# Five instead of four of the eight second-layer steps in split form

## The chip, the cores and the metric

One Trainium2 chip, one of its cores. The program is one launch; the metric is device time in microseconds (us) of that core. Runs of one kernel agree within a few tenths of a per cent; the profile is of one execution.

## The reference

Two parts follow each other. Agent attention: 49 agents attend to 12480 keys (per batch, two batches), and every query attends to the 49 agents. Its output, 24960 rows of 128, goes through a feed-forward layer of 2048 hidden units with ELU.

```python
def _attn_ref(q, k, v, agents):
    a2k = sm(agents, k)              # softmax(scale * a @ b^T)
    agent_v = a2k @ v                # 49 x 128 per batch
    q2a = sm(q, agents)              # 12480 x 49 per batch
    return q2a @ agent_v

def _moe_ref(x, w_in, w_out):
    h = x @ w_in                     # 24960 x 2048
    g = where(h > 0, h, exp(min(h, 0)) - 1)
    return g @ w_out                 # 24960 x 128
```

All is float32; w_in and w_out come as float64.

## The kernel before, in words

`agent_v @ w_in` is folded into a matrix A of 49 rows per batch, so that a hidden value is `p @ A`, with p the query's softmax over the agents. A is kept as a pair of fp32r parts (`ahi`, `alo`), p as well. Queries come in 26 groups (`j`) of 960; each group has two halves of 480, and each half passes through the 2048 hidden units in NP = 8 steps of 256 units (two chunks of 128). That makes S = 416 steps `s`. A *block* is the eight steps of one half: its step number is c = s mod 8 (0 to 7), and its second layer is summed up in one pair of PSUM tiles `o0`, `o1` (`ps_o`, one buffer each).

The work of a step:

- `p1(s)` (L403, TensorE): first layer, three pairs of fp32r matmuls into an `h` slot. Two matmuls of a pair run side by side on the two row halves of the array. There are three `h` slots (`ps_h`); the attention's work takes slots from the same three, in the order in which the program asks for them.
- `elu(s)` (L409, L412, L414): ScalarE writes relu(-h) to `e` (two buffers), then exp of it in place; VectorE makes `g` from `e` and `h`, which sets the `h` slot free.
- `split(s)` (L421, L205), for steps in SPLIT alone: VectorE casts `g` to `hi` (fp32r); GpSimd makes `lo = g - hi` in two halves.
- `p2(s)` (L443, TensorE): second layer. A plain step has two pairs of float32 matmuls, `g` with `w_f`. A split step has six pairs of fp32r matmuls: `hi` with `w_lo` and with `w_hi` (two chunks each), then `lo` with `w_hi`. After step 7, VectorE copies `o1` to `ob` (L455), ScalarE copies `o0` to `oa` (L458), GpSimd adds them (L459).

The order is written out by hand: each engine runs its instructions in the order of the program. In *turn* s of the loop come p1(s), p2(s-4) (LAG = 4; up to turn 5 it is p2(s-3), and turn 6 has none), elu(s), split(s), and then what `pre` lists for that turn. So turn 3 of a block holds the second layer of step 7 of the block before, and turn 4 that of its own step 0. In turn 3 ScalarE's copy `oa` stands between relu and exp of step 3, and VectorE's copy `ob` ahead of `g` of step 3.

The listed attention work: in turn 3 of every second block the scores of the next query group (`q_scores`, L157, with `q_max`, `q_sub`), here called a *score block*; in turn 3 of the blocks between them `q_ring`, the transposes (L328) and the making of `px` (L339, L205), a *ring block*. Both take an `h` slot between those of steps 3 and 4. The sums `z` follow in turns 5 and 6 of a score block, the product `pp` (L324) in its turn 7. In the first seven groups there are two rounds of scores of the second batch's keys per group (`k_round`, turns 13 and 17 of 16), in the next five the sums over v (`ev1`); in about the last thirteen groups only the query work is left.

A prologue of 55 us loads the keys, converts the weights from float64 (`conv`) and computes A of the first batch. There `wo_step`, `wo_hi` and `wo_lo` make `w_hi` and `w_lo` for the steps in SPLIT and `w_f` for the rest.

Of the kernel before, what the change touches and what calls it, by code (L numbers as in the profile page):

```python
# [22 lines left out]
def tile_agent_attention_moe(  # L23
# [24 lines left out]
    LEAD = 6  # L48
    NP = NM // 2
    EDGE = (NP - 1 + LAG) % NP  # L50
    SPLIT = (1, 4, 6, 7)
    PLAIN = tuple(c for c in range(NP) if c not in SPLIT)
    scale = 1.0 / float(C) ** 0.5

# [16 lines left out]
    w_f = big.tile([128, len(PLAIN), 2, 128], F32)  # L71
    w_hi = big.tile([128, len(SPLIT), 2, 128], F32R)
    w_lo = big.tile([128, len(SPLIT), 2, 128], F32R)
    s_all = big.tile([TP, NR, R + 1, NA], F32)
# [123 lines left out]
    def cast_hi(eng, out, x):  # L198
        if eng is nc.scalar:
            nc.scalar.activation(out=out, in_=x, func=ACTF.Copy)  # L200
        else:
            eng.tensor_scalar(out=out, in0=x, scalar1=1.0, scalar2=0.0, op0=ALU.mult, op1=ALU.add)
# [155 lines left out]
    def wo_step(c):  # L358

        if c not in wo_gen:  # L360
            parts = []
            for i in range(2):
                x = 2 * c + i
                y = lambda m, i=i: m[:, 256 * i:256 * i + 256]
                if x in SPLIT:
                    w_e[x] = wc_p.tile([128, 256], F32, tag="even", name="even")
# [8 lines left out]
    def w_part(w, x):  # L375
        return w[:, SPLIT.index(x)].rearrange("p m d -> p (m d)")

    def wo_hi(c):
        for x in (2 * c, 2 * c + 1):
            if x in SPLIT:  # L380
                cast_hi(nc.scalar, w_part(w_hi, x), w_e[x])
# [324 lines left out]
```

## Time and profile before

| what | value |
|---|---|
| time, median of 3 runs | 1029.51 us (1029.46 to 1030.34) |
| the profiled execution's own time | 1029.2 us |
| its span, first to last instruction | 1027.4 us |
| granted TensorE clock, mean | 0.994 |
| TensorE busy in matmuls / weight loads | 98% / 73% |
| ScalarE, VectorE, GpSimd busy | 87%, 80%, 57% |

How to read it: PE is TensorE's matmuls and PEld its weight loads; DVE is VectorE, ACT is ScalarE, POOL is GpSimd. A share is an average over the span. A matmul's end is modelled, so that a recorded duration is longer than the distance to the next matmul; distances are read from starts. In a row of the timeline the first number is the start, the second the length, both in us from the span's start, and what stands in brackets is the idle time of that engine before it and what ended it.

### The profile page before, as it was taken

To read this page: it belongs to the slowest core of one execution; us is meant where nothing else is said; L and a number is where in the kernel's file an instruction comes from. 1 tells how busy PE (TensorE), PEld (TensorE's weight loads), DVE (VectorE), ACT (ScalarE), POOL (GpSimd) and SP (SyncE) were. 2 spreads that over 40 slices of the span, in tenths; PEclk is the share of its full clock that TensorE was granted. 3 is DMA by queue.
4 is the path that set the end of the run, shared out by engine and by line. 5 is a ranking of instruction groups with operands and counts; after the bars stand their busy time and mean duration, and the time that the engine had idled before them with its cause. 6 is when DMAs were issued, how large, how long until landed. Compare 5 with 4: busy or idle time off the path is not lost.

```text
span 1027.4 us, 24745 instructions
## 1 busy us (share of the span) xinstructions
PE 1011.0 (98%) x10138; PEld 753.0 (73%) x10138; DVE 816.9 (80%) x989; ACT 896.4 (87%) x1018; POOL 586.8 (57%) x490
## 2 busy tenths in 40 slices
PE   7999999999999999999999999999999999999998
PEld 5866777777776677776766777777777677777786
DVE  6778787787878777887778888878887887888775
ACT  4588998898898888888889999999999999999995
POOL 3146565565565565566555565656656565656655
PEclk8999999999999999999999999999999999999999
DMA  9921211211222322320110111011011101101000
GB/s 350 368 79 46 93 64 40 84 64 46 78 64 73 89 65 62 100 64 11 55 44 11 54 45 51 14 55 45 22 44 45 54 11 55 45 26 39 25 20 20
DMA packets 25980, 67.27 MB, mean 65 GB/s; under 512 B 3083, under 2 KB 14963, under 8 KB 25867
## 3 DMA queue, kind: packets, MB, share of 16 engines
q1 hardware_dynamic: 25867, 65.69, 19.2%
q8 instruction: 80, 1.31, 0.6%
q14 instruction: 33, 0.27, 0.1%
HBM read 43.11 MB, written 12.78 MB: 54 GB/s over the span
## 4 chain that ended last, share of the span: by engine, by line
PE 92%; DMA 3%; ACT 2%; DVE 2%; issue 1%; SPq 0%; POOLq 0%; POOL 0%; DVEq 0%; ACTq 0%
PE o L443 57%; PE h L403 28%; PE h L157 3%; DMA k<-in_kT_dram 2%; PE h L220 2%; PE h L328 1%; ACT e L409 1%; DMA v<-in_vx_dram 1%; ACT e L412 1%; DVE g L414 1%; PE h L260 0%; DVE m_all L166 0%; PE o L157 0%; DVE ex L96 0%; ACT ex L100 0%
## 5 line engine op out<-in xcount | busy, mean ns | idle before, releaser
L205 POOL TENSOR_TENSOR lo<-g,hi 128x480 fp32r<-128x480 f32 x416 | 511.8, 1252 | 390.2 <-DVE hi L421 231.7
L414 DVE SCALAR_TENSOR_TENSOR g<-e,h 128x960 f32<-128x960 f32 x416 | 478.5, 1153 | 174.5 <-ACT e L412 140.5
L409 ACT ACTIVATE e<-h 128x960 f32<-128x960 f32 x416 | 403.1, 969 | 59.3 <-PE h L403 48.1
L412 ACT ACTIVATE e<-e 128x960 f32<-128x960 f32 x416 | 418.3, 1006 | 11.6
L443 PE MATMUL o<-g,w_f 64*128 64x480 f32 x1664 | 373.6, 562 | 0.0
L403 PE MATMUL h<-py,ahi 49*128 49x480 f32 x832 | 319.7, 463 | 0.7 <-DVE g L414 0.3
L403 PE MATMUL h<-px,ahi 49*128 49x480 f32 x832 | 319.0, 463 | 1.0 <-DVE g L414 0.9
L443 PEld LDWEIGHTS o<-g,w_f 64*128 64x128 f32 x1664 | 169.5, 185 | 91.6 <-issue 80.4
L403 PEld LDWEIGHTS h<-px,ahi 49*128 49x128 f32 x832 | 146.4, 186 | 50.5 <-issue 37.0
L403 PEld LDWEIGHTS h<-py,ahi 49*128 49x128 f32 x832 | 146.4, 186 | 44.6 <-issue 31.7
L421 DVE CAST hi<-g 128x960 fp32r<-128x960 f32 x208 | 171.9, 827 | 7.2
L403 PE MATMUL h<-py,alo 49*128 49x480 f32 x416 | 156.3, 376 | 0.0
L403 PE MATMUL h<-px,alo 49*128 49x480 f32 x416 | 156.2, 376 | 0.0
L443 PE MATMUL o<-hi,w_lo 64*128 64x480 f32 x832 | 130.7, 380 | 0.0
L443 PE MATMUL o<-lo,w_hi 64*128 64x480 f32 x832 | 129.4, 376 | 0.4 <-POOL lo L205 0.4
L443 PE MATMUL o<-hi,w_hi 64*128 64x480 f32 x832 | 128.4, 374 | 0.0
L443 PEld LDWEIGHTS o<-hi,w_lo 64*128 64x128 f32 x832 | 85.9, 185 | 7.6
L443 PEld LDWEIGHTS o<-hi,w_hi 64*128 64x128 f32 x832 | 85.2, 184 | 7.6
L443 PEld LDWEIGHTS o<-lo,w_hi 64*128 64x128 f32 x832 | 85.1, 184 | 7.6 <-POOL lo L205 0.9
L403 PEld LDWEIGHTS h<-px,alo 49*128 49x128 f32 x416 | 76.6, 184 | 4.2
L403 PEld LDWEIGHTS h<-py,alo 49*128 49x128 f32 x416 | 76.6, 184 | 4.1
L459 POOL TENSOR_TENSOR ob<-ob,oa 128x480 f32<-128x480 f32 x51 | 62.1, 1217 | 7.4 <-ACT oa L458 7.4
(86 smaller groups left out, 517.5 us busy)
## 6 DMA issues: line engine op xcount, KB each, us to landing
k<-in_kT_dram SPq DMA_DIRECT2D x26, 480.0 KB
q<-in_qT_dram SPq DMA_DIRECT2D x26, 480.0 KB
out_dram<-ob SPq DMA_DIRECT2D x51, 240.0 KB
py<-px SPq DMA_DIRECT2D x104, 91.9 KB
v<-in_vx_dram SPq DMA_DIRECT2D x13, 516.0 KB
v<-in_vx_dram SPq DMA_DIRECT2D x13, 483.8 KB
raw<-in_w_in_dram SPq DMA_DIRECT2D x4, 512.0 KB
raw<-in_w_out_dram SPq DMA_DIRECT2D x4, 512.0 KB
```

The costliest lines, as they stand in the source:

```text
L157: nc.tensor.matmul(out=ps[u:u + w, j * NA:(j + 1) * NA], lhsT=src[:, x:x + w], rhs=ag_sb[:, b, :], start=True, stop=True)
L205: eng.tensor_tensor(out=out, in0=x, in1=hi.bitcast(F32), op=ALU.subtract)
L220: nc.tensor.matmul(out=ps[u:u + 64], lhsT=e[:, j * NA:j * NA + 64], rhs=v_t[b, r][:, j, :], start=(r == rs[0] and j < 2), stop=(r == rs[-1 ...
L328: nc.tensor.transpose(ps[:NA2, i * TP:(i + 1) * TP], pp[:, i, 0:NA2], ident[:TP, :TP])
L403: nc.tensor.matmul(out=h[:, u, 0:T], lhsT=a[x, :], rhs=p[u ^ half][x, :], start=i == 0, stop=i == 2)
L409: nc.scalar.activation(out=e, in_=h, func=ACTF.Relu, scale=-1.0)
L412: nc.scalar.activation(out=e, in_=e, func=ACTF.Exp, scale=-1.0)
L414: nc.vector.scalar_tensor_tensor(out=g, in0=e, scalar=-1.0, in1=h, op0=ALU.add, op1=ALU.max)
L421: nc.vector.tensor_copy(out=hi_t[s], in_=g_t[s])
L443: nc.tensor.matmul(out=o_t[u][:, 0:T], lhsT=w[x], rhs=v[x, :], start=first and i == 0, stop=last and i == len(jobs) - 1)
L459: nc.gpsimd.tensor_tensor(out=ob, in0=ob, in1=oa, op=ALU.add)
```

## The change

The tuple of the split steps goes from four entries to five. Steps 0 and 5 come in, step 6 goes out; 1, 4 and 7 stay. Nothing else is edited: `PLAIN` (the rest), the sizes of `w_f`, `w_hi`, `w_lo`, the conversions of the prologue, `split` and `p2` follow the tuple.

```diff
@@ -48,7 +48,7 @@
     LEAD = 6
     NP = NM // 2
     EDGE = (NP - 1 + LAG) % NP
-    SPLIT = (1, 4, 6, 7)
+    SPLIT = (0, 1, 4, 5, 7)
     PLAIN = tuple(c for c in range(NP) if c not in SPLIT)
     scale = 1.0 / float(C) ** 0.5
```

## Rows read from the trace of the kernel before

**Rows 1.** The page's first part: busy us, share of the span, instructions of each engine.
```profile
PE 1011.0 (98%) x10138; PEld 753.0 (73%) x10138; DVE 816.9 (80%) x989; ACT 896.4 (87%) x1018; POOL 586.8 (57%) x490
```
**Rows 2.** The timeline of PE, 421 to 435 us: first-layer matmuls of four steps.
```profile
421.79 0.38 PE L403 MATMUL h<-py,alo 49*128 49x480 f32 x1
423.76 0.38 PE L403 MATMUL h<-py,alo 49*128 49x480 f32 x1
...
432.19 0.38 PE L403 MATMUL h<-py,alo 49*128 49x480 f32 x1
434.46 0.38 PE L403 MATMUL h<-py,alo 49*128 49x480 f32 x1
```
**Rows 3.** The timeline, 740 to 743.6 us: turns 3 to 5 of a ring block.
```profile
740.02 0.61 PE L443 MATMUL o<-lo,w_hi 64*128 64x480 f32 x4
740.65 0.57 ACT L458 ACTIVATE oa<-o 128x480 f32<-128x480 f32 x1 [0.32 <-PE o L443]
741.12 1.00 ACT L412 ACTIVATE e<-e 128x960 f32<-128x960 f32 x1
741.15 0.48 PE L403 MATMUL h<-px,ahi 49*128 49x480 f32 x1
741.91 1.78 PE L443 MATMUL o<-g,w_f 64*128 64x480 f32 x8
742.22 1.16 DVE L414 SCALAR_TENSOR_TENSOR g<-e,h 128x960 f32<-128x960 f32 x1 [0.87 <-ACT e L412]
743.49 0.18 PEld L403 LDWEIGHTS h<-px,ahi 49*128 49x128 f32 x1 [0.58 <-issue]
```
**Rows 4.** The timeline of PEld: the same weight load, first and last ring block.
```profile
103.36 0.18 PEld L403 LDWEIGHTS h<-px,ahi 49*128 49x128 f32 x1 [0.57 <-issue]
...
958.04 0.18 PEld L403 LDWEIGHTS h<-px,ahi 49*128 49x128 f32 x1 [0.58 <-issue]
```
**Rows 5.** The timeline, 757.8 to 761.3 us: turns 3 to 5 of a score block.
```profile
757.83 0.62 PE L443 MATMUL o<-lo,w_hi 64*128 64x480 f32 x4
...
759.96 1.77 PE L443 MATMUL o<-g,w_f 64*128 64x480 f32 x8
...
761.29 0.18 PEld L403 LDWEIGHTS h<-py,ahi 49*128 49x128 f32 x1 [0.33 <-issue]
```
**Rows 6.** The timeline of DVE, 768 to 777 us: turn 7, then a ring block's turns 0 to 3.
```profile
768.75 1.16 DVE L414 SCALAR_TENSOR_TENSOR g<-e,h 128x960 f32<-128x960 f32 x1
769.94 1.65 DVE L421 CAST hi<-g 128x960 fp32r<-128x960 f32 x1
771.51 0.56 DVE L324 TENSOR_TENSOR pp<-qe,z 120x392 f32<-120x392 f32 x1
771.99 2.21 DVE L414 SCALAR_TENSOR_TENSOR g<-e,h 128x960 f32<-128x960 f32 x2
774.23 0.66 DVE L421 CAST hi<-g 128x960 fp32r<-128x960 f32 x1
775.27 1.15 DVE L414 SCALAR_TENSOR_TENSOR g<-e,h 128x960 f32<-128x960 f32 x1 [0.38 <-ACT e L412]
776.45 0.66 DVE L455 COPY ob<-o 128x480 f32<-128x480 f32 x1
```
**Rows 7.** The timeline of POOL and ACT in the same stretch.
```profile
768.66 2.41 POOL L205 TENSOR_TENSOR lo<-g,hi 128x480 fp32r<-128x480 f32 x2 [2.05 <-DVE z L318]
...
776.42 0.57 ACT L458 ACTIVATE oa<-o 128x480 f32<-128x480 f32 x1 [0.32 <-PE o L443]
```
**Rows 8.** The timeline, 58 to 63.1 us: the first turns of the loop.
```profile
58.07 1.16 DVE L414 SCALAR_TENSOR_TENSOR g<-e,h 128x960 f32<-128x960 f32 x1 [1.90 <-ACT e L412]
...
63.07 0.48 PE L403 MATMUL h<-px,ahi 49*128 49x480 f32 x1 [0.42 <-DVE g L414]
```
**Rows 9.** The timeline, 1018 to 1022.5 us: the last step.
```profile
1018.41 1.40 DVE L421 CAST hi<-g 128x960 fp32r<-128x960 f32 x1
...
1022.42 0.18 PEld L443 LDWEIGHTS o<-lo,w_hi 64*128 64x128 f32 x2 [0.85 <-POOL lo L205]
```

## The prediction

> **What bounds the kernel now.** I read the page's busy shares first, then the timeline of PE in steps of both kinds, then, where PE's weight loads sat idle, the timelines of the other engines around them. PE has 98% in matmuls, ACT 87%, DVE 80%, POOL 57% [rows 1]. A matmul's recorded end is modelled, so 98% does not yet say that PE never waits; the starts do. From the last first-layer matmul of one step to that of the next it is 423.76 - 421.79 = 1.97 us with a split second layer between them and 434.46 - 432.19 = 2.27 with a plain one [rows 2]. These two distances come back almost everywhere to 0.01 us, so in most turns PE runs at its own pace.
>
> One place is different. I call E the end of the second layer of step 7; it falls in turn 3 of the next block. In the ring block shown E is 740.02 + 0.61 = 740.63. Behind it ACT copies `oa` (740.65 to 741.22), then does exp of step 3 (741.12 to 742.12), then DVE makes `g` of step 3 (742.22 to 743.38), and only 0.11 us after that does the first weight load of step 5 start, at 743.49 after 0.58 us of idle: E + 2.86 [rows 3]. That load needs the `h` slot of step 3, because the ring took the third slot between steps 3 and 4. Meanwhile PE has work until about 741.91 + 1.62 = 743.53 (the plain second layer of step 0 lasts 2.27 less 0.65 of first layer). So gate and work end together: in turn 5 PE stands at the edge of waiting for ACT and DVE. The same load has the same idle time in 23 ring blocks from 103 to 958 us [rows 4]. In a score block E is 757.83 + 0.62 = 758.45 and the load starts at 761.29, E + 2.84; PE is busy until 759.96 + 1.62 = 761.58, 0.29 longer than the gate, because the scores take longer than the transposes [rows 5]; 20 score blocks show this (idle 0.31 to 0.36). The other 8 blocks have sums over v there, or no query work, and room of over half a microsecond.
>
> **The change part by part.**
>
> *TensorE.* Per block one more step is split: 2.27 - 1.97 = 0.30 us less work, 52 x 0.30 = 15.8 us in all if PE did nothing but work [rows 2]. The saving has a place. Step 5 is split now, which makes turn 1 shorter by 0.30; step 6 is plain now, which makes turn 2 longer by as much: nothing. What is left is step 0, whose second layer runs in turn 4, between E and the gate.
>
> In a ring block the gate stands at E + 2.86 whatever PE does, and PE already arrives there with the gate: the saving is 0 in 23 blocks [rows 3, 4]. In a score block PE would be free at 761.58 - 0.30 = 761.28, and the gate with the first matmul is at 761.32. A step that begins after a wait needs 741.91 - 741.15 = 0.76 for its three pairs instead of 0.65 [rows 3]; so 0.30 - 0.04 - 0.10 = 0.16 us is saved, in 20 blocks 3.2 us [rows 5]. In the other 8 it is the whole 0.30, 2.4 us.
>
> *VectorE and GpSimd.* One more cast and two more subtractions per block. A cast alone takes 0.66 us; the one of step 7 took 1.65, because POOL was in the second half of step 6's subtraction (768.66 + 2.41 = 771.07) when the cast came at 769.94, and ended 0.52 after POOL was done [rows 6, 7]. So a cast that meets a running subtraction waits for that half. With 6 plain, step 7's cast meets nothing. But now 7, 0 and 1 are three splits in a row, and 4 and 5 two: the casts of 0, 1 and 5 each come while POOL works on the step before. Where DVE has time this costs nothing; it had 20% of the span [rows 1].
>
> It matters in turns 0 to 3 of a ring block, where `g` of step 2 must be done for the `h` slot of step 4. Before, it ended at 775.27 + 1.15 = 776.42, and E is 776.39 [rows 6, 7]: E + 0.03. After, I go along DVE from turn 7. `g` of step 7 started at 768.75; it will start some 0.55 later (step 5's cast finds half a subtraction, 1.1 with its own 0.66, ahead of the sums; step 6's 0.66 is gone; the rest is slack): 769.3. Then, with durations and overlaps of [rows 6]: g to 770.5, cast 0.66 to 771.2, pp to 771.75, g of step 0 to 772.85, its cast, which comes just behind the start of a second half, 1.55 to 774.4, g of step 1 to 775.5, its cast 0.78 (it meets the last tenths of a first half) to 776.3, g of step 2 to 777.4. E comes 0.16 earlier than before (the score block's saving): 776.23. So g of step 2 ends at E + 1.16, with bounds E + 0.3 (step 0's cast 0.66) and E + 2.0 (step 1's cast 1.65). I take 1.16, since the casts' neighbours are placed by the same rows.
>
> What is late next: step 4's first layer starts at E + 0.52 (741.15) as long as g of step 2 ends by about E + 0.38; at E + 1.16 it starts at E + 1.31, the second layer of step 0 follows 0.76 later and ends 1.31 after that, at E + 3.37. The gate's first matmul was at E + 2.89, with 0.10 for the step behind a wait: 0.38 us late per ring block. This holds for the 12 ring blocks of the last stretch, where the only attention work is the queries': +4.6 us (bounds 0 and 12 x 1.2 = 14). In earlier ring blocks a round of scores or a sum over v lies in turn 0 or 1 and gives PE 0.9 to 1.2 us more work than before E, DVE some 0.3 to 0.6, which covers the lateness; I take 0 there, at most 0.4 x 11 = 4.
>
> *The beginning.* Step 0's second layer, the first of all, now needs `lo`: g of step 0 ends at 59.23, cast to 59.9, two subtraction halves with step 1's cast between them to 62.9, last pair to 63.2, scores to 64.1. Step 4's first layer, at 63.07 before (it waited for g of step 2), comes at 64.2: +1.1 us [rows 8], which the 0.30 of that step is part of. Bounds 0 and 1.6.
>
> *The end.* The last step's cast took 1.40 since it met step 6's subtraction, and PE waited for the `lo` behind it [rows 9]. Step 6 has none now: 1.40 - 0.66 = 0.75 us less. Bounds 0 and 0.85, the wait's length.
>
> *The prologue* makes five pairs of `w_hi` and `w_lo` instead of four: one cast on ACT and one subtraction on POOL more, while the chain there waits for the v that is being loaded. I take 0; at most 1 us.
>
> *Sum* against the profiled execution: 1029.2 - 3.2 - 2.4 + 4.6 + 1.1 - 0.75 = 1028.55. The median of the runs is 0.3 above the profiled execution, so 1028.9 us.
>
> PE has 98% in matmuls but 73% in weight loads, less than ACT's 87% [rows 1]. The Trainium skill, "Perfetto Trace Analysis", section Identifying the Most-Contended Engine, says that matmul busy time is no good measure for TensorE, that weight loads are, and that the engine with the highest occupancy is to be relieved first. By it ACT is that engine, and the change, which relieves TensorE, would give nothing: 1029.5. The gate in turn 5, with ACT's copy and exp in it, agrees in part; the 2.27 and 1.97 us elsewhere don't.
>
> **The rivals.**
>
> 1. *The whole gain.* PE's work is the bound also in turn 4, the gate moves along with it, and 52 x 0.30 arrive: 1029.5 - 15.8 = 1013.7. For it: the regular pace [rows 2]. Against: the gate's links (copy, exp, g) all start from E, which the change doesn't bring nearer [rows 3]. Chance 0.09.
> 2. *The gate, but no lateness*: DVE recovers before E, as it has 20% of idle time, so the 4.6 us fall away: 1024.3. Against: three casts in a row, just where pp lies. Chance 0.18.
> 3. *Slower: the third cast in a row.* If step 1's cast waits for a whole half of step 0's subtraction, g of step 2 ends at E + 2.0 or later, `ob` and g of step 3 move behind it and the gate itself with them. It decides from E + 0.8 on; each 0.1 beyond is 0.1 per block. At 1.2 more it is 12 x 1.2 = 14 us above the forecast, 1043, and with half of it in the 11 earlier ring blocks 1050. For it: casts of 1.65 [rows 6]. Against: DVE's queue itself sets when the cast comes, and two rows of casts can't both hit the worst place. Chance 0.20.
> 4. *ACT is the bound everywhere and PE's work counts for nothing*: 1029.5. Chance 0.08.
>
> **How the numbers follow.** The forecast, gate with a small lateness, has 0.45: 1028.9, by itself from 1025 to 1034 (lateness 0 to 0.7 in 12 blocks, the beginning's and the end's bounds). 0.2% of 1029.5 is 2.1 us; a smaller difference can't be told from none here. Faster by more: all of rival 1, nearly all of 2, 0.05 of the forecast, 0.31. Within: 0.26 of the forecast and rival 4, 0.34. Slower: the rest of the forecast (0.14) and rival 3 with a share of 2, 0.35. The range leaves out rival 1 and the upper half of 3: 1019 to 1045.
>
> **What would show it right or wrong.** In the profile after: starts 1.97 and 2.27 apart in turns 1 and 2, exchanged; in turn 5 of both kinds of blocks the first weight load 0.11 us behind g of step 3, with more idle than 0.58 and 0.33; ring blocks of the last stretch in which step 4's load waits for g of step 2; casts of steps 0 and 5 well over 0.66, of 7 at 0.66. PE's matmul share would fall. I would be wrong if step 5's load no longer follows g of step 3, or if a period of 16 steps in the last stretch is not within 0.5 us of that before.

## The result and the profile after

The kernel with five split steps takes **1037.52 us** (median of 6 runs, 1036.85 to 1038.55), the one before 1029.42 us beside it (6 runs, 1029.09 to 1030.34): a ratio of 1.0079, 95% interval 1.0066 to 1.0092. It is slower by 8.1 us. The forecast was 1028.9, no change.

The profiled execution after took 1038.55 us, with a span of 1036.8; before it was 1029.2 and 1027.4. So 9.4 us of span are to be found. First the page after, its first part and the chain of waits (shares of the span by engine):

```profile
PE 1003.5 (97%) x10346; PEld 772.1 (74%) x10346; DVE 890.4 (86%) x1041; ACT 893.6 (86%) x1019; POOL 732.3 (71%) x595
...
PE 73%; DVE 13%; issue 6%; ACT 4%; DMA 1%; POOL 1%; SPq 0%; DVEq 0%; POOLq 0%; ACTq 0%
```

Against [rows 1], matmuls are busy 7.5 us less, VectorE 73.5 us more, GpSimd 145.5 us more. The chain that ended last was 92% PE and 2% DVE before; now it is 73% and 13%. TensorE waits for VectorE in places where it did not. In which, the list of waits of PE's weight loads says (total us, times, longest), first of the kernel before, then of the one after:

```profile
PEld h L403 <- DVE g L414: 9.2, 35, 1.0
```

```profile
PEld h L403 <- DVE g L414: 28.6, 45, 1.6
...
PEld h L403 <- DVE m_all L166: 5.0, 7, 0.8
```

The table goes by E, the end of step 7's second layer, block by block. Each row is the change of a stretch's length against the kernel before, in us of the profiled executions. The last column is a kernel of the experiments that has the same split steps and the same work as the one after, but has two instructions in another place (e9).

| stretch | forecast | after | e9 |
|---|---|---|---|
| prologue, to the first layer of step 0 (55.07 before) | 0 | +1.1 | +0.3 |
| from there to the first E (79.01) | +1.1 | +2.0 | +0.75 |
| key rounds, to E = 327.02 | -1.1 | +1.8 | -0.65 |
| sums over v, to E = 524.50 | -1.7 | +0.6 | -0.4 |
| last stretch, to E = 972.99 | +2.6 | +5.4 | -2.1 |
| three end blocks and the last step | -1.6 | -1.2 | -1.2 |
| behind the last matmul | 0 | -0.3 | -0.3 |
| sum | -0.7 | +9.4 | -3.6 |

**The last stretch.** The four ends of step 7's second layer, in PE's timeline after (start, length, both in us):

```profile
747.63 0.63 PE L443 MATMUL o<-lo,w_hi 64*128 64x480 f32 x4
...
766.07 0.61 PE L443 MATMUL o<-lo,w_hi 64*128 64x480 f32 x4
...
783.89 0.60 PE L443 MATMUL o<-lo,w_hi 64*128 64x480 f32 x4
...
802.28 0.60 PE L443 MATMUL o<-lo,w_hi 64*128 64x480 f32 x4
```

E is 748.26, 766.68, 784.49 and 802.88. A ring block (E to E) is 18.42 and 18.39 long, where it was 758.45 - 740.63 = 17.82 [rows 3, 5]; a score block is 17.81, where it was 776.39 - 758.45 = 17.94 [rows 5, 6]. So +0.58 and -0.13. Twelve ring blocks give +7.0, twelve score blocks -1.6 (-0.11 to -0.15 each): the +5.4 of the table.

Why a ring block became longer is seen on VectorE. Its timeline after, from turn 5 of the score block to turn 3 of the ring block with E = 784.49 (idle time before it in brackets):

```profile
773.06 1.16 DVE L414 SCALAR_TENSOR_TENSOR g<-e,h 128x960 f32<-128x960 f32 x1 [0.72 <-ACT e L412]
774.25 1.17 DVE L421 CAST hi<-g 128x960 fp32r<-128x960 f32 x1
775.34 0.55 DVE L310 TENSOR_REDUCE z<-qe 120x8 f32<-120x392 f32 x1
775.92 0.91 DVE L315 SCALAR_TENSOR_TENSOR z<-z 120x8 f32<-120x8 f32 x1
776.76 1.14 DVE L414 SCALAR_TENSOR_TENSOR g<-e,h 128x960 f32<-128x960 f32 x1
777.82 0.19 DVE L318 RECIPROCAL z<-z 120x8 f32<-120x8 f32 x1
777.93 1.10 DVE L414 SCALAR_TENSOR_TENSOR g<-e,h 128x960 f32<-128x960 f32 x1
779.07 0.66 DVE L421 CAST hi<-g 128x960 fp32r<-128x960 f32 x1
779.64 0.56 DVE L324 TENSOR_TENSOR pp<-qe,z 120x392 f32<-120x392 f32 x1
780.12 1.14 DVE L414 SCALAR_TENSOR_TENSOR g<-e,h 128x960 f32<-128x960 f32 x1
781.37 1.59 DVE L421 CAST hi<-g 128x960 fp32r<-128x960 f32 x1
782.88 1.14 DVE L414 SCALAR_TENSOR_TENSOR g<-e,h 128x960 f32<-128x960 f32 x1
784.13 0.75 DVE L421 CAST hi<-g 128x960 fp32r<-128x960 f32 x1
784.80 1.14 DVE L414 SCALAR_TENSOR_TENSOR g<-e,h 128x960 f32<-128x960 f32 x1
785.86 0.65 DVE L455 COPY ob<-o 128x480 f32<-128x480 f32 x1
```

POOL in the same stretch, the subtractions of steps 4 and 5 (two halves each):

```profile
772.52 2.39 POOL L205 TENSOR_TENSOR lo<-g,hi 128x480 fp32r<-128x480 f32 x2 [1.96 <-PE h L403]
775.59 2.40 POOL L205 TENSOR_TENSOR lo<-g,hi 128x480 fp32r<-128x480 f32 x2 [0.69 <-DVE hi L421]
```

And the weight load of step 4 that needs the `h` slot of step 2, on PEld:

```profile
785.99 0.18 PEld L403 LDWEIGHTS h<-px,ahi 49*128 49x128 f32 x1 [1.09 <-DVE g L414]
```

Read it from the end. Step 4's load starts at 785.99, E + 1.50, when g of step 2 is done (784.80 + 1.14 = 785.94, E + 1.45). PE has nothing else there. Before, g of step 2 ended at E + 0.03 and step 4's layer started at E + 0.52. Going back, the three casts are 0.66, 1.59 and 0.75, as forecast. The loss lies further up: the sum of `z` (L315), 120 x 8 elements, takes 0.91 us. It starts at 775.92, while POOL is in the first half of step 5's subtraction (775.59 + 1.20 = 776.79), and ends with that half. Over the whole run, first the kernel before, then after (minimum, median and maximum ns):

```profile
L315 DVE SCALAR_TENSOR_TENSOR z<-z x26: 166/167/209, 40.6 to 945.3; 120x8 f32<-120x8 f32 x26
```

```profile
L315 DVE SCALAR_TENSOR_TENSOR z<-z x26: 166/901/924, 41.9 to 957.0; 120x8 f32<-120x8 f32 x26
```

Before, step 5 was plain, and `z` met only the end of step 4's subtraction. POOL and VectorE before, the same turn:

```profile
764.22 2.39 POOL L205 TENSOR_TENSOR lo<-g,hi 128x480 fp32r<-128x480 f32 x2 [3.57 <-DVE hi L421]
...
766.47 0.17 DVE L315 SCALAR_TENSOR_TENSOR z<-z 120x8 f32<-120x8 f32 x1
```

The second half ended at 764.22 + 2.39 = 766.61 and `z` at 766.64: it met only the last 0.14 us, and its 0.17, which it takes alone too, shows no wait. The neighbours in the rows do not lengthen beside POOL: the reduction is 0.55, the reciprocal 0.19, `g` 1.14. The Trainium skill, "SBUF — State Buffer", section SBUF: two separate sides, says that VectorE and GpSimd share a pair of ports as an exclusive lock, held for a whole instruction, and that VectorE asks for it in a two-port mode or with two SBUF inputs. The rows agree: `z` has two SBUF inputs and waits for the rest of the half that it meets; the reduction has one and doesn't.

**The key rounds.** There the maximum of the round (L166) stands behind `z` in turn 5. VectorE after and before, the same turn of the same block:

```profile
166.93 1.20 DVE L421 CAST hi<-g 128x960 fp32r<-128x960 f32 x1
168.05 0.55 DVE L310 TENSOR_REDUCE z<-qe 120x8 f32<-120x392 f32 x1
168.63 0.89 DVE L315 SCALAR_TENSOR_TENSOR z<-z 120x8 f32<-120x8 f32 x1
169.45 0.55 DVE L166 TENSOR_REDUCE m_all<-h 120x49 f32<-120x392 f32 x1
```

```profile
163.54 0.55 DVE L310 TENSOR_REDUCE z<-qe 120x8 f32<-120x392 f32 x1
164.13 0.17 DVE L315 SCALAR_TENSOR_TENSOR z<-z 120x8 f32<-120x8 f32 x1
164.22 0.56 DVE L166 TENSOR_REDUCE m_all<-h 120x49 f32<-120x392 f32 x1
```

The maximum frees the `h` slot that step 0's first layer takes three slots later: it ends at 170.00, and the weight load of that layer comes right behind it, on PEld:

```profile
170.05 0.18 PEld L403 LDWEIGHTS h<-px,ahi 49*128 49x128 f32 x1 [0.78 <-DVE m_all L166]
```

The 7 waits of `m_all` in the list above are this load in seven score blocks from 94 to 322 us, six of them 0.77 to 0.81 long. So five of these score blocks were not 0.16 shorter but 0.11 to 0.14 longer. The sixth is one of two passages to other attention work: the score blocks that begin at E = 307 and 505 in the kernel before became 1.08 and 0.94 longer.

### The profile page after: what moved, and what is told of

Read it like the earlier page. It is cut to its first block, busy times and chain, and to the rows that moved or that the text cites. A ratio compares the mean times of both kernels' runs of the same rounds, so it can differ in the third digit from the quotient of the medians.

```text
span 1036.8 us, 25526 instructions
## 1 busy us (share of the span) xinstructions
PE 1003.5 (97%) x10346; PEld 772.1 (74%) x10346; DVE 890.4 (86%) x1041; ACT 893.6 (86%) x1019; POOL 732.3 (71%) x595
## 4 chain that ended last, share of the span: by engine, by line
PE 73%; DVE 13%; issue 6%; ACT 4%; DMA 1%; POOL 1%; SPq 0%; DVEq 0%; POOLq 0%; ACTq 0%
PE o L443 45%; PE h L403 24%; DVE g L414 9%; PE h L157 3%; ACT e L409 1%; ACT e L412 1%; DVE hi L421 1%; DMA k<-in_kT_dram 1%; DVE s_all L209 1%; POOL lo L205 1%; ACT s_all L212 1%; PE h L220 1%; DVE pp L324 0%; DVE m_all L166 0%; PE h L328 0%
## 5 line engine op out<-in xcount | busy, mean ns | idle before, releaser
L205 POOL TENSOR_TENSOR lo<-g,hi 128x480 fp32r<-128x480 f32 x520 | 656.0, 1287 | 261.7 <-DVE hi L421 172.8
L443 PE MATMUL o<-g,w_f 64*128 64x480 f32 x1248 | 280.8, 562 | 0.0
L421 DVE CAST hi<-g 128x960 fp32r<-128x960 f32 x260 | 246.7, 949 | 16.0
L443 PEld LDWEIGHTS o<-g,w_f 64*128 64x128 f32 x1248 | 130.8, 185 | 64.9 <-issue 58.8
L443 PE MATMUL o<-hi,w_lo 64*128 64x480 f32 x1040 | 164.0, 381 | 0.0
L443 PE MATMUL o<-lo,w_hi 64*128 64x480 f32 x1040 | 161.5, 376 | 1.2 <-POOL lo L205 1.1
L443 PE MATMUL o<-hi,w_hi 64*128 64x480 f32 x1040 | 160.5, 375 | 0.0
L443 PEld LDWEIGHTS o<-hi,w_lo 64*128 64x128 f32 x1040 | 106.9, 185 | 11.5 <-ACT oa L458 0.9
L443 PEld LDWEIGHTS o<-lo,w_hi 64*128 64x128 f32 x1040 | 105.7, 184 | 11.9 <-POOL lo L205 1.9
L443 PEld LDWEIGHTS o<-hi,w_hi 64*128 64x128 f32 x1040 | 105.8, 184 | 10.5
```

Of the source, the lines that this page charges most:

```text
L205: eng.tensor_tensor(out=out, in0=x, in1=hi.bitcast(F32), op=ALU.subtract)
L421: nc.vector.tensor_copy(out=hi_t[s], in_=g_t[s])
L443: nc.tensor.matmul(out=o_t[u][:, 0:T], lhsT=w[x], rhs=v[x, :], start=first and i == 0, stop=last and i == len(jobs) - 1)
```

## The experiments

The theory at the outset (A): the gate of turn 5 takes the gain of step 0's split in ring blocks and half of it in score blocks, as forecast, and what is lost comes from VectorE's lateness behind step 5's cast. The rivals are named with each run. All ratios are to the kernel before, run beside them on the same chip.

**One half of the change: 5 for 6.**

```
-    SPLIT = (0, 1, 4, 5, 7)
+    SPLIT = (1, 4, 5, 7)
```

> Four split steps, 1, 4, 5, 7: step 5 in the place of 6, step 0 plain, so TensorE has the same work as before. Theory A (what costs is DVE's way through turns 5 to 2: step 5's cast meets step 4's subtraction, and behind it the small two-operand sum of z, 0.17 us alone, waits for POOL as well, 0.9): g of steps 6, 7 late as in the changed kernel, but step 0 has no cast, so g of step 2 ends at about E + 0.5 in the last stretch; key rounds: the h slot of a round comes 0.4 us late per score block. Sum 1029.4 + 1 to 4 = 1031 to 1033. Theory B (the loss comes from step 0's cast and the three casts in a row alone): 1029.4, same as before.

Measured 1031.37 us (10 runs), ratio 1.0018 [1.0009, 1.0028]. `z` waits here as well (median 896 ns), yet the blocks of the last stretch are unchanged to 0.03 us, with g of step 2 at E + 0.35. Without step 0's cast between those of 7 and 1, VectorE makes up for the delay before E. In the profiled execution +0.6 came before the first E, +2.1 in the key rounds and the sums over v, most of it at the two passages (+0.57 and +0.95), and -0.7 in the last block.

**The other half: 0 for 6.**

```
-    SPLIT = (0, 1, 4, 5, 7)
+    SPLIT = (0, 1, 4, 7)
```

> Four split steps, 0, 1, 4, 7: step 0 in the place of 6, step 5 plain. TensorE has the same work as before but 0.30 us of it are moved from turn 4, where it waits for g of step 3 anyhow, to turn 2. Theory A (gate in turn 5 at E + 2.86): a ring block gets 0.30 longer, a score block 0.14, so 23 x 0.30 + 20 x 0.14 = 9.7 plus 1 to 2 at the beginning, less 0.75 at the end: 1039 (1037 to 1042); the weight load of step 5 sits idle for about 0.85 in ring blocks. Theory B (TensorE's work is the bound, only casts in a row cost): work as before, casts 7, 0, 1 in a row but no late z: 1029 to 1033.

Measured 1040.28 us (4 runs), 1.0103 [1.0088, 1.0118]. Four split steps as before, so PE's work is the same. Step 6, plain now, costs 0.30 in turn 2 of every block; step 0, split now, gives back nothing in ring blocks (+0.27 to +0.37 in each) and half in score blocks (+0.12 to +0.19 in the regular ones but one, which has +0.51). That is the gate as forecast, measured without any lateness: g of step 2 ends at E + 0.11 and `z` takes 173 ns in the median.

**The sum of z left out, after and before.** The line adds 1e-9 to sums that are at least 1. These two kernels leave out that addition.

```
-            nc.vector.scalar_tensor_tensor(out=z, in0=z, scalar=1e-9, in1=z, op0=ALU.add, op1=ALU.max)
+            pass
```

> The changed kernel without the two-operand sum of z (1e-9 added to a sum that is at least 1, which float32 doesn't hold). Theory A (that sum waits 0.74 us for POOL in each score block behind step 5's cast, and this makes g of step 2 late): in the last stretch g of step 2 ends at E + 0.6 to 0.8 in ring blocks, the 0.58 us lost there go to 0 to 0.1 (12 blocks, 7 us), key rounds' reduce 0.9 earlier (6 x 0.3), the beginning 0.9 less: 1027 to 1030. Theory C (the casts alone fill DVE; the sum only waits where DVE would wait anyhow): 1036 to 1037.5.

> The kernel before without the same sum, as a control. There it takes 0.17 us and meets no subtraction: theories A and C both expect no change, 1029.0 to 1029.6. If it is faster by over 1 us, DVE was a bound before the change too.

After without it (e3): 1027.28 us (10 runs), 0.9978 [0.9969, 0.9988]. Before without it: 1030.1 (10 runs), 1.0005 [0.9996, 1.0015]. One instruction on 960 numbers per query group, 26 times, is worth 10.2 us in one kernel and nothing in the other. In the last stretch of e3 g of step 2 ends at E + 0.52 to E + 0.60, ring blocks are as before to 0.04 but for one with +0.32, score blocks 0.15 shorter. The cast of step 5 still takes 1.20 there, yet g of step 7 starts 3.96 us behind g of step 5 (765.97 to 769.92), as in the kernel before (3.95). So the cast's wait alone makes g of step 7 late by 0.2 us at most (0.01, and the 0.17 of `z` that e3 leaves out); the rest is the wait of `z`. That `z` met no subtraction before, as the control's text has it, was wrong; it met the last 0.1 to 0.2 us of one.

**Is it the second input?** The same sum with one tensor operand:

```
-            nc.vector.scalar_tensor_tensor(out=z, in0=z, scalar=1e-9, in1=z, op0=ALU.add, op1=ALU.max)
+            nc.vector.tensor_scalar(out=z, in0=z, scalar1=1e-9, scalar2=None, op0=ALU.add)
```

> The changed kernel with the sum of z written with one tensor operand (tensor_scalar, add 1e-9) instead of two (the same tile twice). Theory E (it is the second SBUF operand that makes this 120x8 instruction wait 0.74 us for POOL's subtraction): about 0.17 us in all rows, time as without the sum plus 26 x 0.17 us at places where DVE has time: 1027 to 1029. Theory F (any DVE instruction behind step 5's cast waits for POOL): median duration stays at 0.9 us, 1036.5 to 1038.

Measured 1037.09 us (4 runs), 1.0079 [1.0062, 1.0095]: no gain. Its row:

```profile
L315 DVE TENSOR_SCALAR z<-z x26: 173/903/925, 40.6 to 955.5; 120x8 f32<-120x8 f32 x26
```

It waits as long with one tensor input as with two. Which instructions wait for POOL's subtraction can't be told by counting inputs; the two-port mode that the Trainium skill also names in the section above would explain it, but no run here shows the mode.

**The copy `oa` later.** The gate's chain is ScalarE's copy, exp, then g of step 3. With the copy behind the exp it loses a link.

```
         nc.scalar.activation(out=e, in_=h, func=ACTF.Relu, scale=-1.0)
-        if between:
-            between()
         nc.scalar.activation(out=e, in_=e, func=ACTF.Exp, scale=-1.0)
+        if between:
+            between()
```

In three kernels: after without `z`, before, and after with `z`.

> The changed kernel without the two-operand sum of z (as in the run before, 1027.3), and with ScalarE's copy of o0 behind the exp of step 3 instead of between relu and exp. Theory A (step 5's weight load waits for g of step 3, whose exp waits behind that copy for E): g of step 3 ends at E + 1.9 instead of 2.75, the load is no longer bound to it; in score blocks the full 0.30 of step 0 is saved (0.15 more than without this edit, 20 blocks), in ring blocks 0.15 to 0.25 (g of step 2 at E + 0.55 still holds step 4 up by 0.1, and the copy, at E + 1.3, may hold step 0's second layer up by 0.1): 23 x 0.2 + 20 x 0.15 = 7.6 less, 1019 to 1022. Theory D (TensorE is held by something else in turn 5; the copy's place is of no account): 1026.5 to 1028.

> The kernel before with that same move of the copy alone. Theory A: there TensorE's own work ends with the gate, so only some 0.07 us per ring block can be had, and the copy now ends at E + 1.3 where step 0's second layer starts at E + 1.28: 1028 to 1030.5. Theory D: no change. If it is faster by over 3 us, the gate cost the kernel before more than its idle times said.

> The changed kernel with the move of the copy alone, the sum of z kept. Theory A: in ring blocks of the last stretch g of step 2 still ends at E + 1.45 and holds up step 4, so the 0.58 us per block stay lost, less what the step behind it gains; in score blocks 0.15 more is saved (20 blocks), in ring blocks of the earlier stretches 0.2 to 0.3 (11 blocks): 1037.5 - 3.0 - 2.7 = 1032 (1030 to 1034.5), so neither edit alone brings what both bring. Theory D: 1037 to 1038.

After without `z`: 1020.44 us (4 runs), 0.9916 [0.9901, 0.9931]; ring blocks with the gate 0.14 to 0.36 shorter, regular score blocks about 0.31 but for one with +0.44. Before: 1030.37 (10 runs), 1.0014 [1.0004, 1.0023]; there PE's own work ends with the gate or behind it [rows 3, 5], so a nearer gate gives nothing; the three end blocks became 0.5 longer each. After with `z`: 1036.07 (4 runs), 1.0068 [1.0053, 1.0083]. That one fell between the two expectations, 1.6 us above the upper end of the first: score blocks of the last stretch became 0.21 shorter, but ring blocks were still 0.63 to 0.69 longer than before, with g of step 2 at E + 1.52 to E + 1.55. The lateness is not a matter of the gate. The two edits are not additive: 10.2 and 1.5 us apart, 17.1 together.

**The same work in another place.** Leaving `z` out could still be read as relief for a crowded VectorE. So the row sum and `z` were put ahead of step 5's cast, with nothing left out; then the same with the late copy.

```
-    pre = {}
+    pre, mid = {}, {}
...
-            at(s0 + 2, q_sum)
-            at(s0 + 2, q_rz, 0)
+            mid[s0 + 2] = (q_sum, lambda: q_rz(0))
...
                 elu(s, after)
+                for fn in mid.pop(s, ()):
+                    fn()
                 split(s)
```

> The five-of-eight kernel with nothing left out: the row sum and the 120x8 sum z of a query group stand ahead of step 5's cast instead of behind it; the work of each engine is the same, only these three VectorE instructions change their order. Theory G (the price is the place: z is issued while GpSimd's half-subtraction of the same step runs): z lasts 0.17 us instead of 0.90, the cast of step 5 comes some 0.7 us later, when step 4's subtraction is over, and lasts about 0.7 instead of 1.17; g of step 7 starts 0.9 to 1.2 us earlier after g of step 5 than in the five-of-eight kernel, g of step 2 ends by E + 0.6 and the ring blocks of the last stretch lose their +0.57. Time 1026 to 1028.5 us. Rival H (it is not this instruction's place but one more cast and two more subtractions per block, which VectorE has no room for): the wait moves to another instruction, ring blocks keep at least +0.4, time 1034 to 1038.

> The same with ScalarE's copy oa behind the exp of step 3 instead of ahead of it; nothing left out. Theory G: as with z left out and the late copy (1020.4 us), since z then costs 0.17 us in a place where VectorE has room: 1019 to 1022 us. Rival H: as with the late copy alone, 1034 to 1037.

Measured 1025.9 us (10 runs; e9), 0.9972 [0.9954, 0.999], and 1017.82 us (4 runs; e10), 0.9884 [0.9869, 0.9898]. Theory G holds and H falls. Both came out a little below G's range; step 5's cast was wholly freed too (0.65, not 0.7), but that this is the whole reason is not shown. VectorE of the first of them, the same stretch as above:

```profile
763.78 1.15 DVE L414 SCALAR_TENSOR_TENSOR g<-e,h 128x960 f32<-128x960 f32 x1 [0.69 <-ACT e L412]
764.85 0.55 DVE L310 TENSOR_REDUCE z<-qe 120x8 f32<-120x392 f32 x1
765.44 0.24 DVE L315 SCALAR_TENSOR_TENSOR z<-z 120x8 f32<-120x8 f32 x1
765.60 0.65 DVE L421 CAST hi<-g 128x960 fp32r<-128x960 f32 x1
766.16 1.14 DVE L414 SCALAR_TENSOR_TENSOR g<-e,h 128x960 f32<-128x960 f32 x1
767.23 0.19 DVE L318 RECIPROCAL z<-z 120x8 f32<-120x8 f32 x1
767.58 1.15 DVE L414 SCALAR_TENSOR_TENSOR g<-e,h 128x960 f32<-128x960 f32 x1 [0.16 <-issue]
```

From g of step 5 to g of step 7 it is 3.80 us now; after it was 777.93 - 773.06 = 4.87, before 768.75 - 764.80 = 3.95. The instructions and POOL's subtraction are the same; only their order differs. In the last stretch ring blocks are as before to 0.05, score blocks 0.11 to 0.18 shorter (0.16 was forecast): the column e9 of the table.

`z` itself was not back at 0.17 in these two, as theory G had it. First e9, then e10 (minimum, median and maximum ns):

```profile
L315 DVE SCALAR_TENSOR_TENSOR z<-z x26: 166/230/299, 41.0 to 943.4; 120x8 f32<-120x8 f32 x26
```

```profile
L315 DVE SCALAR_TENSOR_TENSOR z<-z x26: 166/448/465, 40.8 to 935.4; 120x8 f32<-120x8 f32 x26
```

That is the same wait in other sizes. In the last stretch `z` starts 1.06 to 1.11 us behind the start of a half of a subtraction in the kernel before and lasts 0.17 to 0.20; in e9 it starts 0.99 to 1.03 behind it and lasts 0.22 to 0.26, in e10 0.78 to 0.81 and 0.45 to 0.46, in the kernel after 0.33 and 0.90 to 0.91. In all four it ends 0.02 to 0.05 us after that half.

With the late copy ring blocks are 0.33 and score blocks 0.31 shorter, as much as the 0.30 of PE's saving, in every block of the last stretch but one ring block (0.08). This version beats both kernels, by 1.16% the one before.

## Why the prediction was wrong

The failing step is one sentence of the walk along VectorE, its term for the delay of g of step 7: g of step 7 "will start some 0.55 later (step 5's cast finds half a subtraction, 1.1 with its own 0.66, ahead of the sums; step 6's 0.66 is gone; the rest is slack)". The cast's length was right, 1.17. But the sums behind it were carried over with their durations from the kernel before, and their surroundings had changed: step 5's own subtraction starts soon after its cast is done, and `z` falls into its first half. Measured, g of step 7 starts 4.87 - 3.95 = 0.92 later, not 0.55, and nearly all of it goes with `z`: without `z`, and with the cast still at 1.20, it starts 0.01 later (e3). So two errors stood in the term. Of the 0.55 laid to the cast at most 0.2 came, and the 0.74 by which `z` grew was put at nothing; that the term came as near as it did was luck. From there to g of step 2 the walk was right: 8.01 us (777.93 to 785.94), forecast 8.1. So g of step 2 ended at E + 1.45 instead of E + 1.16, and a ring block lost 0.58 instead of 0.38. The prediction saw that a cast waits for a running subtraction; it did not ask the same of the other VectorE instructions whose place beside POOL was new.

One count was also wrong: the gate stands in 19 score blocks, not 20, since the load of the first, behind E = 79.01, comes 1.19 us after g of step 3; 9 blocks, not 8, are without it. The sum changes by less than 0.2 us.

Point by point:

- *The gate in turn 5*: right. Nothing in ring blocks, -0.16 forecast and -0.11 to -0.15 measured in the score blocks of the last stretch; the run with 0 for 6 and e9 show it without the lateness. Step 5's load still follows g of step 3 by 0.116 us in ring blocks to E = 293 and in score blocks of the last stretch. But its idle time did not grow, as I had said: 0.52 for 0.58 and 0.30 for 0.33.
- *Turns 1 and 2*: exchanged as said. After, the last first-layer matmuls are 1.97 apart in turn 1 and 2.27 in turn 2:

```profile
778.57 0.37 PE L403 MATMUL h<-py,alo 49*128 49x480 f32 x1
780.54 0.38 PE L403 MATMUL h<-py,alo 49*128 49x480 f32 x1
782.81 0.38 PE L403 MATMUL h<-py,alo 49*128 49x480 f32 x1
```

- *Lateness of the last stretch*: 12 x 0.38 = +4.6 forecast, 12 x 0.58 = +7.0 measured. That a late g of step 2 holds up step 4's load was right; what makes it late was not. With `z` left out or moved (e3, e9) the loss is zero but for one block of e3: g of step 2 ends at E + 0.44 to E + 0.60 there, once at E + 0.79, not at the walk's E + 1.16.
- *Score blocks of the key rounds and the passages*: the sign was wrong, +1.8 for -1.1 in that stretch and two passages of about +1. The cause is again `z`, here through the maximum that stands behind it; with `z` out of the way (e3, e9) the regular score blocks show -0.14 to -0.18 and the passages -0.09 to +0.17. One score block of e3, to E = 138 before, has +0.46; `z` is left out there, so this has another cause, which stays open.
- *The 8 blocks without a gate*: -2.4 forecast, of which about -0.8 came, also in e9. In the blocks with sums over v, g of step 2 ended at E + 0.63 to E + 0.85 in the kernel after and step 4's load waited for it; that these blocks have cover was wrong.
- *The beginning*: +1.1 forecast for step 4's wait. It is +1.08 in e3; after has 0.9 more, since `z` also waits in the first score block (73.62 to 74.54).
- *The end*: right. The last cast is 0.66 as forecast. The last block is 0.88 shorter, with what step 0 gives in it; with 5 for 6 alone, where step 0 is plain, it is 0.75 shorter, the forecast.

```profile
1028.87 0.66 DVE L421 CAST hi<-g 128x960 fp32r<-128x960 f32 x1
```

- *The prologue*: 0 forecast, +1.1 in the profiled execution after. In e3 the loop also begins 1.1 later, in e9 and e10, which make the same five pairs, 0.3 and 0.1, and in two other kernels with five pairs no later than before. So it is not a fixed price of the fifth pair; what makes it differ stays open.

Of the rivals, the third had the side right (slower, VectorE late in turn 3) but not the place: it laid it on step 1's cast, which took 0.75, near the forecast's 0.78. Rival 2, the gate without lateness, is what the change does once `z` stands elsewhere: 1025.9 measured, 1024.3 forecast. Rivals 1 and 4 fell: e10 shows that the whole gain in the regular blocks needs the gate's chain shortened as well.

## What to carry to other kernels

When a change gives GpSimd work at a new time, list every VectorE instruction that now falls into it, however small, and price each from a row where it stands beside such work; a duration from another place is no bound, even if it stood beside such work there: before, `z` met only the end of a subtraction. A short instruction that waits delays all behind it in its queue, and what it costs is set by the next deadline on that queue, here the `h` slot of step 2. Here, moving it ahead of the cast that GpSimd's subtraction waits for turned a loss of 8.1 us into a gain of some 3 (0.28%), with nothing left out.

## What the runs showed of the hardware that was not expected

A VectorE sum of 120 x 8 float32 elements took 0.17 us alone and 0.90 us when it started 0.33 us into a GpSimd subtraction of 128 x 480 (1.22 us), with two tensor inputs and with one alike (901 and 903 ns in the median). Started later into such a subtraction it took less, and it ended 0.02 to 0.05 us after the subtraction in the kernels before, after, e9 and in the last stretch of e10, so its length there was set by what was left of GpSimd's instruction. It did not wait for the next subtraction that was already queued (776.83, while the second half ran to 777.99). A reduction from 120 x 392 to 120 x 8 (0.55), a reciprocal of 120 x 8 (0.19) and `g` (1.14) kept their length beside the same subtraction.
